# A recurrence and its mixture of experts on one core: half of the products of v moved between two PE groups, a DRAIN of GpSimd before the last four scatters, and the last output group in two column halves

## The chip, the core and the metric

One NeuronCore of a Trainium2 chip runs the whole kernel. The metric is device time in microseconds of one execution. The kernel before took 394.21 us (median of 11 runs, 393.25 to 394.7).

PE is TensorE (PEld its weight loads), DVE is VectorE, ACT is ScalarE, POOL is GpSimd, SP is SyncE. A letter q behind an engine's name (POOLq, SPq) means its sequencer: waits, branches, drains and DMA issues, which are not counted as busy time.

## The reference

A gated linear recurrence feeds a top-1 mixture of experts. Everything is float32.

```python
# q, k, v, f_logit: (4, 8, 768, 48)
f = 1.0 / (1.0 + np.exp(-f_logit))
for t in range(S):
    state = f[:, :, t, :, None] * state + np.einsum('bhd,bhe->bhde', k[:, :, t], v[:, :, t])
    y[:, :, t] = np.einsum('bhd,bhde->bhe', q[:, :, t], state)
# y -> x of (3072, 384); w_gate (384, 8), w1 (8, 384, 1024), w2 (8, 1024, 384)
...
logits = x @ w_gate
expert_idx = np.argmax(logits, axis=1)
...
h = np.maximum(x_sorted[lo:hi] @ w1[e], 0.0)
y_sorted[lo:hi] = h @ w2[e]
...
return (gate_w[:, None] * y).astype(np.float32)
```

So each of 3072 tokens gets 384 values from the recurrence, picks one of 8 experts, passes that expert's two layers, and its row is scaled by its gate and written to its own place in the output.

## The kernel before, in words

**The recurrence** is cut into chunks of 128 tokens; 12 units (`NU`) of two batch halves each are taken through a software pipeline, the loop `for n in range(1, NU + 2)`. In step `n` the unit `here = n` gets its scores, `back = n - 1` gets its outputs and `last = n - 2` is turned into token rows. The whole kernel is recorded under a manual schedule: the order in which the code emits instructions is the order in which each engine runs them. In a steady step PE runs, in this order:

- `score` (L529): 16 products k by q of unit n, into `s`
- `keys` (L544): 8 transposes of k of unit n, into two PSUM tiles `kp`; ACT copies them to `kn` (`keep`, L549)
- `rows` (L649): 8 products of the finished outputs `ys` of unit n-2 with a selection matrix, into two PSUM tiles `xp`. The tiles of `kp`, `xp` and `dp` come from two buffers used in turn (`turns`), so the first `xp` can only start when ACT has copied the first `kp`. DVE then sums the gate logits from `xp` (L657), and ACT copies the rows out (`lay`, L674 and L679)
- `within` (L557), called for `a = 0` and `a = 1`: 8 products each of masked scores `at` and `v` of unit n-1, into `yt`
- `added` (L594): 16 products of v and `kn`, into `dp`
- `before` (L578): 16 products of q and the old state, into `yt`

Beside PE, per step, DVE masks the scores (L535), scans the log decays (L477, `sum`), sums logits (L657), scales q (L518), does the routing (L214 to L260) and adds the state (L611). ACT copies `yt` out (`settle`, L619), takes exponentials and logs (L462, L470, L491, L506) and lays the rows. POOL scales k (L495), scales the state (L613), and issues the scatters of rows into the DRAM tensor `xs` (L189), sorted by expert. Every float32 product is two passes on PE, so 8 products show as 16 MATMUL records.

**The experts** follow: for each expert, a wide layer (L316, `hps`, with ReLU on ACT L326 or DVE L328) and a narrow one (L332, `yps`), in tiles of 128 tokens; DVE scales each finished tile by the gate (L344, `ysb`) and POOL scatters its 128 rows into the output (`put`, L339; `scatter`, L189). Overflowing tokens are packed into quads, four groups of 32 tokens of four experts, whose products (L1091) use four 32-column strips of PE side by side. The last expert ends in this order: the tile that rides with a quad (`narrow_riding`), the load of the last quad's second weights (`quad_second`), DVE's 16 transposes for the last quad (`turn_quad`, L1084), two plain tiles (`narrow_late`), and the last quad (`narrow_quad` with `last` set), whose gate scaling is shared by DVE (columns 192 to 383, L344) and ACT (columns 0 to 191, L346), before one scatter of it.

**The end**: a register is loaded (L1151) and a branch (L1152) skips the fallback code. POOL's sequencer then runs INC_SWDGE_SEM (L1152) and a DRAIN (L1300); SP's waits for all semaphores, the last scatter's among them (L1300); then all engines meet in two barriers.

Of the kernel before, what the change touches and what calls it, by code (L numbers as in the profile page):

```python
# [10 lines left out]
F32 = mybir.dt.float32  # L11
I32 = mybir.dt.int32
U8 = mybir.dt.uint8
AF = mybir.ActivationFunctionType
# [11 lines left out]
NU = B // 2 * NC  # L26
# [99 lines left out]
def kernel(  # L126
# [211 lines left out]
            )  # L338
        put(x, t, yp, group)  # L339

    def put(x, t, yp, group, last=False):
        ysb = ep.tile([128, DM], F32, name="ysb")
        gate, half = x["tg"][:, t, 1:2], DM // 2 if last else 0
        nc.vector.tensor_scalar(ysb[:, half:], yp[:, half:], gate, None, op0=OP.mult)  # L344
        if last:
            nc.scalar.activation(ysb[:, 0:half], yp[:, 0:half], AF.Copy, scale=gate)  # L346
        scatter(out, x["dst"][:, t : t + 1], ysb, N - 1, group)


    ordered = {getattr(mybir.EngineType, n) for n in ENGINES}  # L350
# [56 lines left out]
    with ExitStack() as st:  # L407
# [107 lines left out]
        def by_decay(u, part=whole):  # L515
            x = units[u]
            q = x["q"][:, part]
            nc.vector.tensor_tensor(q, q, x["dec"][:, part], op=OP.mult)  # L518
# [270 lines left out]
        for n in range(1, NU + 2):  # L789
            here, back, last = n, n - 1, n - 2  # L790
            ahead = n + 1 < NU
            state = n < NU - 2
            rt = None
            if here < NU:
                units[here]["old"] = states[here % 2]
            if 2 <= last:
                settle(last)
            if later and later[0] < NU - 1:
                later[1].weigh()
            if here < NU:  # L800
                for a in range(2):
                    score(here, a)
            if ahead and n != 2:
                by_r(n + 1)
                ends(n + 1)
            if decayed:
                decayed()
                decayed = None
            if sends:
                scatter_some(n)  # L810
            if n == NU - 2:
                soon = [load_rows(first[e]) for e in range(EARLY)]
            if n == 1:
                units[0]["old"] = None
                added(0)
                update(0)()
            if ahead and not 1 < n < 4:
                decay(n + 1)
                last_decay(n + 1)
            if state:  # L820
                keys(here)
                keep(here)
            if n == 2:
                growth(n + 1)
                by_r(n + 1)
                ends(n + 1)
            if 1 < n < 4:
                decay(n + 1)
                last_decay(n + 1)
            if here < NU:  # L830
                for a in range(2):
                    for h in range(2):
                        mask(here, a, h)
            if n == 1:
                log(3)
                within(0, 0)
                within(0, 1)
                settle(0)
            if n + 3 < NU:
                steps(n + 3)  # L840
            if later and n >= NU - 1:
                settled(*later)
                later = None
                scatter_some(NU)
            if 2 < n < NU - 2:
                total(n + 2)
            if n == NU - 2:
                by_decay(n + 1)
            if 0 <= last:
                rt = rows(last, later[1] if later else None)  # L850
                lay(last)
            if later and n == NU - 2:
                settled(*later)
                later = None
                scatter_some(NU)
            if ahead and n < NU - 2:
                by_decay(n + 1)
            if n == 2:
                total(n + 2)
            if rt:  # L860
                rt.choose()
                if n < NU - 2:
                    routed.append(rt.latest)
                if n >= NU - 1:
                    rt.weigh()
            if later:
                settled(*later)
                routed.append(later[1].latest)
                later = None
            for a in range(2):  # L870
                if 0 < back < NU:
                    within(back, a)
            if n == 2:
                settle(1)
            if n + 2 < NU and n != 1:
                growth(n + 2)
            if n == NU + 1:
                widen(soon[0], weights[0], early_h, range(3, 7))
            if n == NU:
                turn_early(soon[0])  # L880
            if state:
                added(here)
                decayed = update(here)
            if n == 1:
                total(3)
            if back < NU:
                before(back)
            if rt:
                later = (n, rt)
                if n >= NU - 1:  # L890
                    rt.count(turns("rp", [128, 2, rt.n, E]))
                if n >= NU:
                    settled(*later)
                    later = None
            if n == NU:
                early_h = early_banks()
                widen(soon[0], weights[0], early_h, range(3))
            if n == NU + 1:
                widen(soon[0], weights[0], early_h, range(7, NF))
                turn(soon[1])  # L900
            if n == 1:
                load(n + 3, "q")
            if n + 3 < NU:
                load(n + 3, "k")
            if n + 2 < NU:
                load(n + 2, "v")
            if 1 < n and n + 3 < NU:
                load(n + 3, "q")
            if n + 5 < NU:
                load(n + 5, "f")  # L910
            if n == 1:
                load_first_pads()
            if n in (8, 10):
                load_first_weights((n - 8) // 2)
                load_second_weights((n - 8) // 2)
# [106 lines left out]
    with ExitStack() as st:  # L1022
# [27 lines left out]
        def quad_second(q, g):  # L1050
            quads[q]["second"][g] = w2 = qp.tile([128, NF, DM], F32, name="qw2", bufs=4)
            quad_weights(w2, q, g, moe_w2, W2)
# [30 lines left out]
                for j, to in pieces():  # L1083
                    nc.vector.transpose(x["hT"][to, :, r], hq[r, j])  # L1084

        def narrow_pieces(parts, x, t, last=False):

            yp = psz.tile([128, DM], F32, name="yps")
            for f in range(NF):
                for (g, r), (h, at, w) in zip(pieces(), parts):  # L1090
                    nc.tensor.matmul(  # L1091
                        yp[r],
                        lhsT=h[:, f, at : at + T],
                        rhs=w[:, f],
                        start=f == 0,
                        stop=f == NF - 1,
                        skip_group_check=True,
                    )
            put(x, t, yp, "out", last)

        def narrow_quad(x, last):
            narrow_pieces([(x["hT"], g * T, x["second"][g]) for g in range(4)], x, 0, last)

        def narrow_riding(x, w, ridden, g):

            t = TILES - 1
            parts = [(x["hT"], t * C + j * T, w[1]) for j in range(3)]
            narrow_pieces([*parts, (ridden["hT"], g * T, ridden["second"][g])], x, t)

        quads = [None] * QUADS  # L1110

# [8 lines left out]
        for e in range(E):  # L1120
            x, w = rows_of[e], weights[e]
            end = e == E - 1
            x["hT"] = qp.tile([128, NF, TILES * C], F32, name="hT")[:, :, 0 : x["rows"]]
            widen(x, w, bank, range(NF))
            if e in WITH:
                widen_quad(quads[WITH[e]])
            if e + 1 < E:
                turn(rows_of[e + 1])
            if e + 1 in WITH:
                turn(quads[WITH[e + 1]], qp)  # L1130
            if e + 2 < E:
                rows_of[e + 2] = load_expert(e + 2)
                load_first_weights(e + 2)
            fetch(2 * e)
            if e in WITH and not end:
                turn_quad(quads[WITH[e]])
            if end:
                narrow_riding(x, w, quads[0], RIDE[e])
                quad_second(1, 3)
                turn_quad(quads[WITH[e]])  # L1140
            for t in range(TILES - 1 if e in RIDE else x["n"]):
                narrow_late(x, t, w)
            if end:
                narrow_quad(quads[WITH[e]], True)
            elif e in RIDE:
                narrow_riding(x, w, quads[0], RIDE[e])
            if e + 2 < E:
                load_second_weights(e + 2)
            fetch(2 * e + 1)
# [155 lines left out]
```

## Time and profile before

| what | value |
|---|---|
| runs shown | 394.21 us median, 393.25 to 394.7 |
| profiled execution | 394.03 us, span of its instructions 392.2 us |
| mean granted TensorE clock | 0.992 |
| busy: PE, PEld, DVE, ACT, POOL | 375.7, 263.3, 168.5, 103.1, 113.5 us |
| 25 scatters into the output, POOL | 971 ns each |
| 24 scatters into `xs`, POOL | 1293 ns each on average |

The profile gives instructions in groups (line, engine, operation, output and inputs, shapes), each group's busy time, its mean duration and the idle time of its engine before it with what ended that. `[0.24 <-ACT kn L549]` behind a row of the timeline says that the engine stood idle for 0.24 us and that ACT's copy into `kn` ended that. PE ends are modelled; PE starts are recorded. The recurrence takes the first 120 us or so, the experts the rest.

### The profile page before, as it was taken

What the parts mean: (1) busy time and instruction counts of PE and PEld (TensorE: products, weight loads), DVE (VectorE), ACT (ScalarE), POOL (GpSimd) and SP (SyncE); (2) the same over time, 40 slices, a digit from 0 to 9 for tenths busy, and PEclk for the clock granted to TensorE, in tenths of its full rate; (3) what the DMA queues carried; (4) which work ended last, traced back from release to release, by engine and by line L of the source; (5) the groups of instructions that cost most, each with busy time, mean ns of one, the idle gap of its engine ahead of it and who ended that gap; (6) DMA issues with size and microseconds to landing.
All of it is one profiled execution on the core that took longest, in us unless ns stands there. A gap on an engine that the chain in (4) does not pass through costs nothing. (4 is left out here: it accounts for less than half of the span.)

```text
span 392.2 us, 7597 instructions
## 1 busy us (share of the span) xinstructions
PE 375.7 (96%) x2998; PEld 263.3 (67%) x2998; DVE 168.5 (43%) x362; ACT 103.1 (26%) x191; POOL 113.5 (29%) x117
## 2 busy tenths in 40 slices
PE   7889999999999999999999999999999999999991
PEld 7778889999989778685555555655466466464440
DVE  6899988888664632112121131117312113011540
ACT  6998877785432101010100000010010010011000
POOL 5378867787617400100001001000200100100010
PEclk9999999999999999999999999999999999999996
DMA  7999667778759559694669799897182379991320
GB/s 273 390 375 345 229 206 250 238 238 287 277 161 357 182 147 330 147 345 77 195 203 353 237 390 395 214 399 189 40 293 63 99 274 389 406 403 51 117 106 24
DMA packets 51484, 95.05 MB, mean 242 GB/s; under 512 B 20802, under 2 KB 40696, under 8 KB 49392
## 3 DMA queue, kind: packets, MB, share of 16 engines
q1 hardware_dynamic: 48016, 84.76, 64.2%
q0 software_dynamic: 3136, 9.64, 6.5%
q8 instruction: 25, 0.41, 0.4%
q14 instruction: 19, 0.16, 0.1%
q10 hardware_dynamic: 288, 0.08, 0.1%
HBM read 79.46 MB, written 15.21 MB: 241 GB/s over the span
## 5 line engine op out<-in xcount | busy, mean ns | idle before, releaser
L316 PE MATMUL hps<-xT,w1t 128*128 128x352 f32 (+2 forms) x384 | 110.1, 447 | 0.0
L316 PEld LDWEIGHTS hps<-xT,w1t 128*128 128x128 f32 x384 | 72.7, 190 | 37.2 <-issue 1.9
L332 PE MATMUL yps<-w2t,hT 128*128 128x384 f32 x288 | 94.4, 487 | 0.0
L189 POOL DMA_INDIRECT out_dram<-ysb,dst x25 | 24.3, 971 | 229.1 <-DVE ysb L344 224.2
L332 PEld LDWEIGHTS yps<-w2t,hT 128*128 128x128 f32 x288 | 54.6, 190 | 38.5 <-issue 1.5
L326 ACT ACTIVATE hT<-hps 128x352 f32<-128x352 f32 (+2 forms) x28 | 13.7, 490 | 200.7 <-PE hps L316 190.6
L328 DVE TENSOR_SCALAR hT<-hps 128x352 f32<-128x352 f32 (+2 forms) x28 | 15.6, 558 | 93.0 <-PE hps L316 93.0
L344 DVE TENSOR_SCALAR ysb<-yps,tg 128x384 f32<-128x384 f32 x22 | 13.6, 618 | 74.5 <-PE yps L332 55.8
L189 POOL DMA_INDIRECT xs<-xr,posi x24 | 31.0, 1293 | 16.7 <-DVE place L245 9.6
L535 DVE COPY_PREDICATED at<-mpack,s 128x512 f32<-128x512 uint8 x48 | 31.0, 725 | 9.4 <-PE s L529 9.4
L495 POOL TENSOR_TENSOR k<-k,r 128x1024 f32<-128x1024 f32 (+1 forms) x12 | 26.5, 2212 | 22.1 <-ACT r L491 10.4
L477 DVE TENSOR_TENSOR_SCAN sum<-g,cap 128x1032 f32<-128x1032 f32 (+1 forms) x14 | 28.7, 2053 | 3.0 <-ACT g L470 3.0
L649 PE MATMUL xp<-fpack,ys 128*128 128x104 f32 x192 | 25.2, 281 | 2.6 <-ACT kn L549 2.4
L1091 PE MATMUL yps<-qw,hqT 128*32 128x384 f32 x128 | 26.7, 488 | 0.0
L529 PE MATMUL s<-q,k 64*128 64x128 f32 x384 | 24.7, 278 | 2.1 <-POOL last L513 1.5
L649 PEld LDWEIGHTS xp<-fpack,ys 128*128 128x128 f32 x192 | 22.7, 192 | 4.8 <-ACT kn L549 4.3
L529 PEld LDWEIGHTS s<-q,k 64*128 64x128 f32 x384 | 22.4, 188 | 4.0 <-POOL last L513 1.6
L557 PE MATMUL yt<-at,v 128*48 128x128 f32 x384 | 23.5, 275 | 0.0
L1091 PE MATMUL yps<-w2t,hT 128*32 128x384 f32 x192 | 21.4, 487 | 0.0
L557 PEld LDWEIGHTS yt<-at,v 128*48 128x48 f32 x384 | 20.4, 123 | 1.3 <-issue 0.2
L518 DVE TENSOR_TENSOR q<-q,g 128x1024 f32<-128x1024 f32 (+1 forms) x14 | 16.7, 1196 | 0.5 <-DMA q<-in_qu_dram 0.5
L619 ACT COPY ys<-yt 128x512 f32<-128x512 f32 x24 | 12.9, 591 | 14.2 <-PE yt L578 14.2
(113 smaller groups left out, 351.6 us busy)
## 6 DMA issues: line engine op xcount, KB each, us to landing
qw<-in_moe_w_dram SPq DMA_DIRECT2D x16, 1536.0 KB, 12.8
w1t<-in_moe_w_dram SPq DMA_DIRECT2D x8, 1536.0 KB, 6.8
w2t<-in_moe_w_dram SPq DMA_DIRECT2D x8, 1536.0 KB, 14.3
k<-in_ku_dram SPq DMA_DIRECT2D x12, 512.0 KB, 5.4
q<-in_qu_dram SPq DMA_DIRECT2D x12, 512.0 KB, 4.9
f<-in_fu_dram SPq DMA_DIRECT2D x11, 512.0 KB, 6.1
xs<-pad SPq DMA_DIRECT2D x8, 600.0 KB, 4.3
v<-in_vu_dram SPq DMA_DIRECT2D x12, 384.0 KB, 5.3
```

The source lines that it names most:

```text
L189: ins = nc.gpsimd.indirect_dma_start(out=dst, out_offset=bass.IndirectOffsetOnAxis(ap=idx, axis=0), in_=src, in_offset=None, bounds_check= ...
L316: nc.tensor.matmul(x["h"][:, f], lhsT=w[0][:, j, b * 128 : b * 128 + 128], rhs=x["xT"][:, j], start=j == 0, stop=j == KD - 1,)
L328: nc.vector.tensor_scalar(to, x["h"], 0.0, None, op0=OP.max)
L332: nc.tensor.matmul(yp, lhsT=x["hT"][:, f, t * C : t * C + C], rhs=w[1][:, f, :], start=f == 0, stop=f == NF - 1,)
L477: nc.vector.tensor_tensor_scan(x["sum"][:, part].rearrange("p s c -> p (s c)"), x["g"][:, part].rearrange("p s c -> p (s c)"), cap[:, part ...
L495: ins = on.tensor_tensor(k, k, units[u]["r"][:, part], op=OP.mult).ins
L518: nc.vector.tensor_tensor(q, q, x["dec"][:, part], op=OP.mult)
L529: nc.tensor.matmul(ps[h][:, p], lhsT=x["k"][r, s], rhs=x["q"][r, s], start=True, stop=True)
L535: nc.vector.copy_predicated(x["at"][:, a, h], _bc(causal, 1, HP), x["ps", a][h])
L557: nc.tensor.matmul(x["yt"][DP * (h ^ a) : DP * (h ^ a) + D, a, p], lhsT=x["v"][:, a, 2 * p + h], rhs=x["at"][:, a, h, p], start=p == 0, st ...
L649: nc.tensor.matmul(xp[:, p], lhsT=x["ys"][:, a, p], rhs=wx[:, p, 0:XW] if a else wx[:, p, E:WX], start=True, stop=True,)
L1091: nc.tensor.matmul(yp[r], lhsT=h[:, f, at : at + T], rhs=w[:, f], start=f == 0, stop=f == NF - 1, skip_group_check=True,)
```

## The change

Three edits. (1) In steps 2 to 9 `within(back, 0)` is called after `keys`, ahead of `rows`, and `within(back, 1)` stays where both were. (2) A plain DRAIN is put in POOL's stream behind the scatter of the last riding tile, ahead of the four scatters that then remain (two plain tiles and two halves). (3) The last quad is multiplied in two column halves of 192, each with its own PSUM tile, its own gate scaling on DVE, its own SBUF tile (`ysh`, a pair of buffers) and its own scatter into the output seen as 6144 rows of 192; ACT's part is gone. The two lists of destinations (`dst2`) are made by two small DVE operations just ahead of the 16 transposes of `turn_quad`. No instruction of SP is added or moved.

```diff
-    def put(x, t, yp, group, last=False):
+    def put(x, t, yp, group):
         ysb = ep.tile([128, DM], F32, name="ysb")
-        gate, half = x["tg"][:, t, 1:2], DM // 2 if last else 0
-        nc.vector.tensor_scalar(ysb[:, half:], yp[:, half:], gate, None, op0=OP.mult)
-        if last:
-            nc.scalar.activation(ysb[:, 0:half], yp[:, 0:half], AF.Copy, scale=gate)
+        nc.vector.tensor_scalar(ysb, yp, x["tg"][:, t, 1:2], None, op0=OP.mult)
         scatter(out, x["dst"][:, t : t + 1], ysb, N - 1, group)
+
+    HD = DM // 2
+    out_halves = out.rearrange("n (h d) -> (n h) d", h=2)
+
+    def halves_of(x, t):
+
+        x["dst2"] = ep.tile([128, 2], I32, name="dst2", bufs=1)
+        with nc.allow_low_precision("whole numbers"):
+            for h in range(2):
+                nc.vector.tensor_scalar(
+                    x["dst2"][:, h : h + 1], x["tg"][:, t, 0:1], 2.0, float(h), op0=OP.mult, op1=OP.add
+                )
+
+    def put_half(x, t, h, yp, group):
+        ysb = ep.tile([128, HD], F32, name="ysh")
+        nc.vector.tensor_scalar(ysb, yp, x["tg"][:, t, 1:2], None, op0=OP.mult)
+        scatter(out_halves, x["dst2"][:, h : h + 1], ysb, 2 * N - 1, group)
...
+            first_half = 1 < n < NU - 2
+            if first_half:
+                within(back, 0)
             if 0 <= last:
                 rt = rows(last, later[1] if later else None)
                 lay(last)
...
-            for a in range(2):
+            for a in range(int(first_half), 2):
                 if 0 < back < NU:
                     within(back, a)
...
-        def narrow_pieces(parts, x, t, last=False):
-
-            yp = psz.tile([128, DM], F32, name="yps")
+        def narrow_pieces(parts, yp, cols=slice(0, DM)):
...
-                        rhs=w[:, f],
+                        rhs=w[:, f, cols],
...
-        def narrow_quad(x, last):
-            narrow_pieces([(x["hT"], g * T, x["second"][g]) for g in range(4)], x, 0, last)
+        def narrow_quad(x):
+            parts = [(x["hT"], g * T, x["second"][g]) for g in range(4)]
+            for h in range(2):
+                yp = psz.tile([128, DM], F32, name="yps")[:, 0:HD]
+                narrow_pieces(parts, yp, slice(h * HD, h * HD + HD))
+                put_half(x, 0, h, yp, "out")
...
             if end:
                 narrow_riding(x, w, quads[0], RIDE[e])
+                nc.gpsimd.drain()
                 quad_second(1, 3)
+                halves_of(quads[WITH[e]], 0)
                 turn_quad(quads[WITH[e]])
             for t in range(TILES - 1 if e in RIDE else x["n"]):
                 narrow_late(x, t, w)
             if end:
-                narrow_quad(quads[WITH[e]], True)
+                narrow_quad(quads[WITH[e]])
```

More of the change, by code (lines that the diff above doesn't have):

```diff
@@ L1098, in narrow_pieces @@
                     )
-            put(x, t, yp, "out", last)
-        def narrow_quad(x, last):
-            narrow_pieces([(x["hT"], g * T, x["second"][g]) for g in range(4)], x, 0, last)
+        def narrow_quad(x):
[4 more added lines that the diff above has]
+                put_half(x, 0, h, yp, "out")
         def narrow_riding(x, w, ridden, g):
@@ L1107, in narrow_riding @@
             parts = [(x["hT"], t * C + j * T, w[1]) for j in range(3)]
-            narrow_pieces([*parts, (ridden["hT"], g * T, ridden["second"][g])], x, t)
+            yp = psz.tile([128, DM], F32, name="yps")
+            narrow_pieces([*parts, (ridden["hT"], g * T, ridden["second"][g])], yp)
+            put(x, t, yp, "out")
         quads = [None] * QUADS
```

## The prediction, made before the changed kernel ran

> **What bounds the kernel now.** I read the page first, then the list of waits, then one steady step of the recurrence in the timeline, then the end. PE is the bound nearly everywhere:
>
> ```profile
> PE 375.7 (96%) x2998; PEld 263.3 (67%) x2998; DVE 168.5 (43%) x362; ACT 103.1 (26%) x191; POOL 113.5 (29%) x117
> ...
> PE   7889999999999999999999999999999999999991
> ```
>
> Only the first slices and the last one are open. In the list of waits PE's largest wait between those is the one that edit 1 aims at:
>
> ```profile
> PE xp L649 <- ACT kn L549: 2.4, 8, 0.7
> ```
>
> Eight times in the recurrence, 2.4 us in all, the row products stand until ACT has copied the transposed keys. One steady step, number 7:
>
> ```profile
> 73.33 2.59 DVE L535 COPY_PREDICATED at<-mpack,s 128x512 f32<-128x512 uint8 x4 [1.35 <-PE s L529]
> ...
> 74.12 1.09 PE L544 MATMUL kp<-fpack,k 128*128 128x128 f32 x8
> ...
> 75.45 2.03 PE L649 MATMUL xp<-fpack,ys 128*128 128x104 f32 x16 [0.24 <-ACT kn L549]
> ...
> 77.42 1.96 PE L557 MATMUL yt<-at,v 128*48 128x128 f32 x32
> 78.03 0.26 DVE L657 TENSOR_REDUCE lg<-xp 128x8 f32<-128x32 f32 x2
> 78.21 1.21 DVE L518 TENSOR_TENSOR q<-q,g 128x1024 f32<-128x1024 f32 x1
> ...
> 79.20 1.09 PE L594 MATMUL dp<-v,kn 128*64 128x48 f32 x32
> ...
> 80.75 2.36 POOL L495 TENSOR_TENSOR k<-k,r 128x1024 f32<-128x1024 f32 x1 [1.28 <-DVE ex L222]
> 81.24 0.94 PE L529 MATMUL s<-q,k 64*128 64x128 f32 x12
> ```
>
> The step is 9.1 us from score to score (72.14 to 81.24), PE stands for 0.24 of it, and DVE (1.35) and POOL (1.28) wait longer than that: PE sets the pace. The end:
>
> ```profile
> 378.07 5.37 PE L1091 MATMUL yps<-qw,hqT 128*32 128x384 f32 x64
> ...
> 383.51 0.42 DVE L344 TENSOR_SCALAR ysb<-yps,qtg 128x192 f32<-128x192 f32 x1 [4.71 <-PE yps L1091]
> 383.96 0.42 ACT L346 ACTIVATE ysb<-yps,qtg 128x192 f32<-128x192 f32 x1 [23.41 <-DVE ysb L344]
> 384.66 0.97 POOL L189 DMA_INDIRECT out_dram<-ysb,dst  x1 [4.61 <-ACT ysb L346]
> ```
>
> ACT's half runs behind DVE's, not beside it. After PE's last pass (383.44) there are still 8.7 us, and the chain view, which knows no sequencers, stops at the last scatter. What follows is in the source view of the program's last line and of the scatter:
>
> ```profile
> L1300 POOLq DRAIN  x3: 40/248/4077, 386.8 to 391.9; - x3
> ```
> ```profile
> DMA to landing us min/median/max: 4.1/4.1/4.1
> ```
>
> The first line: POOL's sequencer begins a DRAIN at 386.80 that takes 4.08 us, to 390.88; the barriers behind it end at 392.17, 1.29 later. The second: the last scatter landed 4.1 after its start, at 388.73; the two before it took 2.6 each. SP works off its waits 0.98 after that landing (389.71). So POOL's DRAIN ends last, by 1.17, and SP's wait for the last landing is the next limit.
>
> **Edit 1, the products of v.** Sixteen passes go from behind the row products to before them. I count by PE starts in the single records. Now: last key transpose to first row pass 0.51; row to v passes 0.205; 32 v passes 1.68 from first to last start; 0.10 to the next group. Together 2.495. After: transposes to v passes 0.20 (as in step 1, where they stand so); 16 v passes 0.79 (seven pair steps of 0.111); v to row passes unknown, 0.20 like other changes of tile shape; 0.205; 0.79; 0.10. Together 2.285: **0.21 a step**. Here a rule speaks against the edit: the Trainium skill, "TensorEngine Tiling (Array Packing)", Key Properties, says that a change of tiling mode drains TensorE. The trace prices it: row passes follow transposes of the same shape at 0.11, and a change of shape costs 0.20. There are two more changes per step. Without the rule the edit would give 0.40 a step; with it 0.21; if the unknown one cost 0.4 instead, nothing.
>
> In steps 2 and 3 the gain goes elsewhere: there `dp` waits for ACT's copy of the rows (33.17 after 0.50, 41.85 after 0.38), in step 2 because ACT has no gap before it, in step 3 because DVE hasn't. PE arrives earlier and waits longer: zero. So six steps, 4 to 9: **1.27 us**. Bounds: 0 and 2.4 (all of the wait). What is late next: the rows end 0.69 later within a step. In steps without routing counts that ends just at DVE's scan (to 78.11), costing DVE 0.1; in those with counts, 0.5. DVE's waits before its masks are 0.93 to 1.46, and POOL's before k at least 1.28, so this is covered. Its price when not is a rival below. From 120 us on PE has no wait above 0.2, so the gain reaches the end. The masks of unit n-1 and v lie a step back, and `settle` of `yt` ends at 73.35, before the new place at 75.2.
>
> **Edit 3, halves.** PE: 128 passes of 192 columns for 64 of 384. The last quad's four strips step at 0.322 for 384 columns. Four-strip groups at 128 columns (L578) step at 0.11, so 192 columns should step at about 0.165, 32 steps: 5.3 against 5.15 now, within 0.1. Per four, 0.13 of weight loads fits inside. Both ends: 5.15, and 10.3 if a step stayed at 0.322; I take the near one because 128 columns already run at a third. DVE and POOL for the first half fall at about 381 to 382.6, beside PE. Their PSUM tiles are freed by DVE at 376 and 378.8, in time. For the second: PE ends at 383.44, DVE 0.42 at 383.51, POOL 0.28 after DVE as before: the last scatter starts at **384.21 instead of 384.66**. ACT's half and its handover are gone. The two small DVE operations (0.13 each by the casts L305) delay the transposes by 0.26; they end at 375.4 and PE wants them at 378.07.
>
> **Edit 2, the DRAIN.** First its own time: POOL has 6.77 idle between the riding tile's scatter (ends 369.56) and the next (376.33). If the DRAIN waits for that scatter's landing (374.74), or takes 4.08 from 369.6, it is over before 376. It has no releasers and no user. Were it stretched as scatters are beside DVE (2.33 instead of 0.97) it would end at 379.4, pushing two scatters by 3 and 1 us, whose landing nobody waits for before 386. So zero, up to about 15 us.
>
> Then the last DRAIN. What makes it 4.08 no row says outright. Three more DRAINs on POOL: 0.19 at the start, no DMA issued yet; 0.25 and 0.04 right after the long one, POOL idle in all. So the time belongs to what happened since the previous DRAIN: 49 scatters, 0.083 each. It isn't the last landing, which came 2.15 before its end. If it is work per scatter, four remain: 0.33. If it is a fixed price once any scatter was issued, 4.08 stays. The rule: the Trainium skill, "VectorE: DVE Perf Modes", section "The DRAIN you can't avoid", counts DRAINs of pre- and postamble as about 12 ns boilerplate on all engines. SP's rows agree (7 to 13 ns), POOL's row exceeds it 340 times, so the row decides. By the rule there is nothing to win here; by the row up to 3.7.
>
> **The sum at the end.** Last scatter 384.21, landing 2.6 later (the two rows before it; the 4.1 of the last one had one packet behind a 16 KB instruction fetch from 386.04 to 387.67 on its ring, and the new packets start at 385.75, ahead of that): 386.81. POOL: scatter to 385.18, INC_SWDGE_SEM 1.16, a DRAIN of 0.3 or until the landing: 387 at most. SP: 386.81 + 0.98 = 387.79, which is now the later. Plus 0.04 and 1.29: 389.12, **3.05 less** than 392.17. With 1.27: 4.32. The profiled execution was 394.03 (span 392.17 and 1.86 around): 389.71. It lies 0.18 below the median of the runs, so **389.9**.
>
> **Rivals.** (a) The DRAIN is shortened, but the last landing again meets an instruction fetch and takes 4.1: plus 1.5, 391.4. For it: fetches come as engines reach the end, which moves little against the scatter. (b) The DRAIN's price is fixed: POOL ends 386.37 + 4.08 + 1.29 = 391.74, 0.43 less, with edit 1 1.7: 392.5. For it: nothing counts the scatters in any row; against: the short ones right behind. (c) Slower: the rows' delay of 0.69 passes through DVE (logits, q, state) into the next score, in every step from 2 to 9. That costs 8 x 0.69 = 5.5 instead of gaining 1.27: 394.21 - 3.05 + 5.5 = 396.7. It decides from 0.5 a step on, (3.05 + 0.8) / 8; against it stands the 0.93 and more that DVE waits for PE now. (d) The change doesn't do what it says: DRAIN fixed and the shape changes eat edit 1: 0.43, 393.8.
>
> **Chances.** Forecast 0.50 (389.2 to 390.7), (a) 0.18, (b) 0.18, (c) 0.07, (d) 0.07. A difference of 0.2% (0.8 us) is about what this kernel's runs can tell from none. Faster: forecast, (a), (b), 0.86; within: (d), 0.07; slower: (c), 0.07. The range 389.1 to 392.9 holds the first three with their spread.
>
> **What would show it.** Edit 1: the wait of `xp` for `kn` gone, steps 4 to 9 at 8.9 instead of 9.1, PE's 120 us mark 1.3 earlier. Edit 3: the halves end 5.2 to 5.4 after their start, last scatter 0.77 after PE. Edit 2: a DRAIN of some 4 to 5 us near 370 and under 1 us at the end. I am wrong if the last DRAIN is still 4, if steps stay at 9.1, or if the halves take far over 5.4.

## The result and the profile after

The changed kernel takes **390.11 us** (median of 8 runs, 389.79 to 390.56) against 394.21 for the kernel before beside it (31 runs): a ratio of 0.9899, 95% interval 0.9888 to 0.9911, so 3.5 to 4.4 us less. Its profiled execution took 390.09, its span 388.3, at a granted clock of 0.996.

The page's busy row and its slices of PE:

```profile
PE 375.9 (97%) x3062; PEld 264.6 (68%) x3062; DVE 168.5 (43%) x365; ACT 103.0 (27%) x190; POOL 113.8 (29%) x118
...
PE   7889999999999999999999999999999999999993
```

PE is as busy as before (375.7), in 64 more records; the last slice went from a tenth to three, since less lies behind PE's end. PE's list of waits (engine, line, for whom: us in all, times, longest):

```profile
PE yt L708 <- DVE gsum L433: 2.1, 1, 2.1
PE s L543 <- POOL last L527: 1.4, 1, 1.4
PE xp L663 <- DMA fpack<-in_moe_w_gate_dram: 1.1, 1, 1.1
PE dp L608 <- ACT xr L693: 0.8, 1, 0.8
PE s L543 <- POOL rend L515: 0.5, 1, 0.5
PE xp L663 <- ACT ys L633: 0.2, 1, 0.2
```

The eight waits of `xp` for `kn` are gone. What is left comes once each, at the start of the recurrence or at its end; `dp` waits 0.83 in step 3 for ACT's rows, where 0.38 stood before. Step 7 in the timeline:

```profile
72.61 2.62 DVE L549 COPY_PREDICATED at<-mpack,s 128x512 f32<-128x512 uint8 x4 [0.60 <-PE s L543]
73.41 0.86 PEld L558 LDWEIGHTS kp<-fpack,k 128*128 128x128 f32 x8
73.41 1.09 PE L558 MATMUL kp<-fpack,k 128*128 128x128 f32 x8
...
74.43 1.08 PE L571 MATMUL yt<-at,v 128*48 128x128 f32 x16
...
75.14 2.28 DVE L491 TENSOR_TENSOR_SCAN sum<-g,cap 128x1032 f32<-128x1032 f32 x1
75.24 3.04 POOL L189 DMA_INDIRECT xs<-xr,posi  x1 [0.15 <-issue]
...
75.44 2.03 PE L663 MATMUL xp<-fpack,ys 128*128 128x104 f32 x16
...
77.41 1.08 PE L571 MATMUL yt<-at,v 128*48 128x128 f32 x16
...
80.19 2.37 POOL L509 TENSOR_TENSOR k<-k,r 128x1024 f32<-128x1024 f32 x1 [0.30 <-DVE ex L222]
80.35 0.49 PE L543 MATMUL s<-q,k 64*128 64x128 f32 x4
```

From score (71.42) to score (80.35) the step takes 8.93 instead of 9.10, without a gap on PE. The slack that covered the edit has shrunk: DVE waits 0.60 before its masks instead of 1.35, POOL 0.30 before `k` instead of 1.28. In step 9, 0.17 is left of DVE's 0.93. The end of the timeline:

```profile
376.07 0.97 POOL L189 DMA_INDIRECT out_dram<-ysb,dst  x1 [7.86 <-issue]
...
376.72 5.41 PE L1107 MATMUL yps<-qw,hqT 128*32 128x192 f32 x128
...
379.60 0.42 DVE L360 TENSOR_SCALAR ysh<-yps,qtg 128x192 f32<-128x192 f32 x1 [2.15 <-PE yps L1107]
380.29 0.97 POOL L189 DMA_INDIRECT out_dram<-ysh,dst  x1 [1.60 <-DVE ysh L360]
382.20 0.42 DVE L360 TENSOR_SCALAR ysh<-yps,qtg 128x192 f32<-128x192 f32 x1 [2.18 <-PE yps L1107]
382.89 0.97 POOL L189 DMA_INDIRECT out_dram<-ysh,dst  x1 [1.63 <-DVE ysh L360]
```

PE ends at 382.13 (383.44 before), and the last scatter starts 0.76 later. The two DRAINs, in the source views of their lines (duration min/median/max in ns, then first and last start), and the landing of the two half scatters, in the view of tile `ysh`:

```profile
L1160 POOLq DRAIN  x1: 8202/8202/8202, 367.0 to 367.0; - x1
```
```profile
L1323 POOLq DRAIN  x3: 46/249/2039, 384.2 to 388.0; - x3
```
```profile
DMA to landing us min/median/max: 2.2/2.7/3.1
```

The new DRAIN takes 8.20, not 4. The last one takes 2.04 instead of 4.08: it starts at 384.17, the last scatter lands (the last of the 16 counts of its semaphore comes) at 385.99, 3.1 after the scatter's start, and the DRAIN ends at 386.20, 0.21 behind that landing. SP has worked off its waits at 387.04, so SP, by way of the landing, now ends last, and the barriers behind it end at 388.32.

Where the 3.85 us of span went: 1.31 ahead of PE's end, 2.54 behind it (8.73 before, 6.19 after). Of the 1.31, 0.38 was there at the first score of the pipeline already (9.93 and 9.55), ahead of any edit. Steps 0 to 2 added 0.11, and step 3 took 9.98 instead of 9.70 with the wait of `dp`, a loss of 0.28 that the repeat below doesn't have (9.69). So at the score of step 4 the changed kernel was 0.21 ahead (43.95 and 43.74); in the repeat, whose first score came at 9.20, it was 0.01 ahead (43.94). Steps 4 to 9 gave 0.17 each, 1.02, and the rest came behind them.

### The profile page after: what moved, and what is told of

It reads as the page before. It is cut to its first block, busy times and chain, and to the rows that moved or that the text cites. A ratio compares the mean times of both kernels' runs of the same rounds, so it can differ in the third digit from the quotient of the medians.

```text
span 388.3 us, 7726 instructions
## 1 busy us (share of the span) xinstructions
PE 375.9 (97%) x3062; PEld 264.6 (68%) x3062; DVE 168.5 (43%) x365; ACT 103.0 (27%) x190; POOL 113.8 (29%) x118
## 4 chain that ended last, share of the span: by engine, by line
PE 89%; DMA 5%; SPq 1%; DVE 1%; ACT 1%; issue 1%; POOL 0%; POOLq 0%; ACTq 0%
PE hps L316 28%; PE yps L332 24%; PE yps L1107 7%; PE xp L663 6%; PE yt L571 5%; PE s L543 5%; PE s L316 3%; PE hps L1081 3%; PE yp L332 3%; PE yt L592 3%; PE dp L608 2%; DMA fpack<-c_fpack 2%; PE kp L558 2%; DMA f<-in_fu_dram 2%; DMA fpack<-in_moe_w_gate_dram 2%; SPq L466 1%
## 5 line engine op out<-in xcount | busy, mean ns | idle before, releaser
L189 POOL DMA_INDIRECT out_dram<-ysb,dst x24 | 23.3, 972 | 224.4 <-DVE ysb L343 216.3
L189 POOL DMA_INDIRECT xs<-xr,posi x24 | 32.3, 1347 | 16.6 <-DVE sums L235 9.2
L1107 PE MATMUL yps<-qw,hqT 128*32 128x192 f32 (+1 forms) x192 | 26.8, 380 | 0.0
L571 PE MATMUL yt<-at,v 128*48 128x128 f32 x384 | 25.1, 277 | 0.0
L1107 PEld LDWEIGHTS yps<-w2t,hT 128*32 128x32 f32 x192 | 7.6, 110 | 13.0 <-issue 12.5
```

The lines of the kernel that those rows point to most:

```text
L189: ins = nc.gpsimd.indirect_dma_start(out=dst, out_offset=bass.IndirectOffsetOnAxis(ap=idx, axis=0), in_=src, in_offset=None, bounds_check= ...
L571: nc.tensor.matmul(x["yt"][DP * (h ^ a) : DP * (h ^ a) + D, a, p], lhsT=x["v"][:, a, 2 * p + h], rhs=x["at"][:, a, h, p], start=p == 0, st ...
L1107: nc.tensor.matmul(yp[r], lhsT=h[:, f, at : at + T], rhs=w[:, f, cols], start=f == 0, stop=f == NF - 1, skip_group_check=True,)
```

## Experiments

Two things were open. **Edit 1**: how much of the gain is its own, and is it covered by slack. **The DRAIN**: the forecast read 4.08 us as 49 scatters at 0.083 each, but the new DRAIN with 46 scatters behind it took 8.20. My first theory for that: it waits for the last landing and then takes 0.043 per scatter (386.80 to 390.88 holds both). Rivals: 0.083 per scatter from its own start, stretched by DVE's transposes beside it in the new place; or a fixed price.

The first and the third batch ran on two chips whose granted TensorE clock falls to 0.5 for 7 to 10 us near 122 us in all eight kernels profiled there (in two of them, the first run of edit 1 alone and both halves ahead, also for 3.4 us, from 31.3 and from 35.5), and the kernel before takes 403.9 and 403.74 us there. So times are compared within a batch, and the tail (from PE's last end to the span's end) across batches. The changed kernel itself was run only where there is no such fall.

**Edit 1 alone** (first batch)

```diff
--- before
+            first_half = 1 < n < NU - 2
+            if first_half:
+                within(back, 0)
...
-            for a in range(2):
+            for a in range(int(first_half), 2):
```

> Only the move of the first half of the products of v (edit 1). Theory of the record: steps 4 to 9 each 0.17 to 0.21 us shorter, nothing in steps 2 and 3: 394.2 - 1.0 to 1.3 = 392.9 to 393.2. Rival: the profile of the changed kernel has step 3 longer by 0.28 us and a start that was 0.4 us earlier by itself; if the move causes the longer step 3, the gain is 0.7 or less: 393.5. The end of the kernel is as before: the DRAIN of 4 us sets it.

403.87 us, ratio 0.9989 (0.9974 to 1.0004); tail 8.74. A gain of at most 1 us, and none shown: the 1.0 to 1.3 that were expected aren't there. Its even steps are 9.38 as in the changed kernel, but steps 5, 7 and 9 are 9.23 to 9.28 instead of 8.93: the 32 passes of `before` (L578, `yt<-q,state`) take 1.1 to 1.2 from first to last start instead of 0.82.

**Edit 2 alone** (first batch)

```diff
--- before
                 narrow_riding(x, w, quads[0], RIDE[e])
+                nc.gpsimd.drain()
                 quad_second(1, 3)
```

> Only the DRAIN ahead of the last expert's remaining scatters (three here, edit 2). Theory now: a DRAIN waits for the last scatter's landing and then takes about 0.043 us for each scatter since the DRAIN before (before: 2.15 us after the landing for 49; changed: 1.92 for 46, 0.21 for 4). The last one then ends 0.15 to 0.25 us after the landing, SP's waits 1.0 after it, and the end comes 1.1 us earlier: 393.1. Rival, the record's reading: 0.083 us for each scatter from its own start; the same end, but the DRAIN in the middle takes 3.8 us, not 8. Rival, a fixed price: 394.2.

402.88, ratio 0.9973 (0.9953 to 0.9993); tail 7.61, 1.12 shorter. The line of its last DRAIN, in the source view:

```profile
L1301 POOLq DRAIN  x3: 46/249/3054, 395.5 to 400.4; - x3
```

It still has 3.05, but as a wait for the landing (398.37, 0.17 ahead of its end), which now sets the end through SP.

**Edit 3 alone** (first batch)

```diff
--- changed kernel
-            first_half = 1 < n < NU - 2
+            first_half = False
...
-                nc.gpsimd.drain()
```

> Only the last quad in two column halves (edit 3), no DRAIN and no move. The last scatter starts 0.45 us earlier. Theory now (landing, then 0.043 us for each of 50): the DRAIN at the end still takes long and ends 2.15 us after the last landing, so the whole gain of the landing counts, 0.45 plus what the landing itself gets shorter (4.1 down to 2.6 to 3.1): 1.4 to 1.9, 392.3 to 392.8. Rival, the record's 0.083 for each scatter from the DRAIN's own start: only the earlier start counts, 0.45, 393.8.

403.65, ratio 0.9989 (0.9968 to 1.0009); tail 8.36, 0.37 shorter.

```profile
L1322 POOLq DRAIN  x3: 40/249/4158, 395.9 to 401.1; - x3
```

Fifty scatters, 4.16 us from its start at 395.91 to 400.07. The counts of the last scatter's semaphore, kept in the trace, put its landing at 396.98: a landing followed by 0.043 per scatter would have ended the DRAIN at 399.13, 0.94 sooner. That theory falls here.

**Edits 1 and 3** (first batch)

```diff
--- changed kernel
-                nc.gpsimd.drain()
```

> The changed kernel without its DRAIN. Theory now: the last DRAIN again ends about 2.15 us after the last landing, SP's waits 1.05 after it, so 1.1 us slower than the changed kernel: 391.2. Rival: the DRAIN buys nothing (its price is fixed, or the landing sets the end anyway): 390.1. Rival 0.083 us from its own start: the DRAIN would begin near 384.2 and end at 388.3, where the changed kernel's ended at 386.2: 391.3, not to be told apart by the time, but by the DRAIN's end against the landing.

403.48, ratio 0.9983 (0.9965 to 1.0001); tail 8.36, DRAIN 4.16 again, 2.80 of it behind the landing. The second miss of that theory.

**The changed kernel again** (second batch, before 393.91)

> The changed kernel once more, beside the others on one chip. Theory now: the DRAIN takes 0.083 us for each scatter since the DRAIN before, from its own start, and ends no earlier than 0.2 after the last landing (49 scatters 4.08, 50 scatters 4.16, wherever the landing was). So 1.1 us or a little more less than without its DRAIN, and 3 to 4 us less than before. Rival: on the chip of the single edits the steps 5, 7 and 9 lost 0.3 us each in the products with the old state, with edit 1 only; if that is the chip's doing, edit 1 is worth 0.2 to 0.4 there and the changed kernel only 2 to 2.5 us less than before.

390.46 (390.16 to 391.21), ratio 0.9912 (0.9897 to 0.9928); tail 6.32. The result repeats, with 3.45 between the medians instead of 4.10.

**Edits 2 and 3** (second batch)

```diff
--- changed kernel
-            first_half = 1 < n < NU - 2
+            first_half = False
```

> The changed kernel without edit 1 (DRAIN and halves alone). Theory: the tail gain of 2.5 to 3.0 us alone, so 391.2 to 391.7 where before is 394.2, and 1.0 slower than the changed kernel beside it. Rival: edit 1 is worth nothing or 0.3, then it is within 0.3 of the changed kernel. DRAIN without halves gave 0.8 to 1.1 and halves without DRAIN 0.35 to 0.45; if these were all, the pair would give 1.2 to 1.5; the theory has more for the pair, since without the long DRAIN the earlier landing counts too.

391.98, ratio 0.9942 (0.9924 to 0.9961); tail 6.35. Against the changed kernel beside it edit 1 is worth 0.0030 of the ratio, 1.2 us, or 1.5 by the medians; steps 9.55 and 9.10 against 9.38 and 8.93 account for 1.02. The two intervals just touch, so the runs alone leave the size of it loose.

**The DRAIN far ahead, 26 scatters left** (second batch)

```diff
--- changed kernel
         over, okc = share(), sums()
+        nc.gpsimd.drain()
...
-                nc.gpsimd.drain()
```

> The changed kernel with its DRAIN at the end of the recurrence instead, behind the 24 scatters into xs, so that 26 scatters are left for the last one. Theory (0.083 each, from its own start, not before the landing): the last DRAIN takes 26 x 0.083 = 2.16, starts 1.3 after the last scatter and ends 3.5 after its start, about 0.4 after a landing at 3.1; SP's waits end 1.05 after the landing, so the time is that of the changed kernel. Rival (landing, then 0.043 each): DRAIN ends 1.1 after the landing, no more than 0.1 slower. Rival (two prices, 4 us when anything is left from the recurrence's scatters, else 0.3): also the time of the changed kernel, but the DRAIN ends with the landing plus 0.2. The first DRAIN, 24 scatters: 2.0 of work, or until the landing of the last row plus 0.2.

391.0, ratio 0.9928 (0.991 to 0.9947), which the runs can't tell from the changed kernel beside it; tail 6.14.

```profile
L1323 POOLq DRAIN  x3: 46/248/2368, 385.3 to 388.7; - x3
```

It starts at 385.33, the last scatter lands at 386.59, it ends at 387.70: 1.11 after the landing, 0.043 for each of 26. By 0.083 from its own start it would have been 387.49; in the changed kernel (four scatters) the end follows the landing by 0.21, in the long new DRAINs (46) by 1.93. The new DRAIN of this kernel has 24 scatters behind it:

```profile
L1014 POOLq DRAIN  x1: 7839/7839/7839, 129.6 to 129.6; - x1
```

It takes 7.84 where 2.0, or the landing and 0.2, were expected: the landing comes at 136.44, and it ends 1.03 later, 0.043 for each of 24.

**The DRAIN away from the transposes, edit 1 in steps 4 to 9 only** (second batch)

```diff
--- changed kernel
-            first_half = 1 < n < NU - 2
+            first_half = 3 < n < NU - 2
...
+            if end:
+                nc.gpsimd.drain()
             x["hT"] = qp.tile([128, NF, TILES * C], F32, name="hT")[:, :, 0 : x["rows"]]
...
-                nc.gpsimd.drain()
```

> The changed kernel with edit 1 in steps 4 to 9 alone, and the DRAIN at the start of the last expert, 45 scatters behind it and 5 ahead, where DVE makes no transposes. Theory: in the changed kernel the DRAIN in the middle ended 1.9 us after the landing because DVE's 16 transposes ran beside it; here its 45 x 0.083 = 3.7 us are over before the landing (7 us after the scatter), and it ends within 0.3 of it. Rival: it ends 1.9 after the landing here too (45 x 0.042 after it). Time: edit 1 gave nothing in steps 2 and 3 but 0.3 more in step 3, so 0 to 0.3 faster than the changed kernel; the earlier DRAIN changes nothing at the end.

390.29 (389.93 to 390.62), ratio 0.9903 (0.9887 to 0.9919); tail 6.13.

```profile
L1145 POOLq DRAIN  x1: 9086/9086/9086, 342.4 to 342.4; - x1
```

With DVE nearly idle (busy for 1.05 of these 9.1 us) and 45 scatters behind it, the DRAIN takes 9.09 and ends 1.89 after the landing. So the transposes have no part in its length. Leaving steps 2 and 3 as before makes no difference that shows (390.29 against 390.46).

What fits all of these DRAINs, as a sum and not as something that a row shows: **two passes of about 0.0415 us per scatter issued since the last DRAIN, and the second starts only when the last of them has landed**, so end = later of (start + 0.0415 n, landing) + 0.0415 n. Before: 386.80 + 2.03 = 388.83, just behind the landing at 388.73, + 2.03 = 390.86 (measured 390.88). The walk of 0.083 from its own start fits there only because the landing came within the first half. Every scatter here has 128 rows, so a price per scatter and a price per row can't be told apart; the size of a row doesn't show (49 scatters of whole rows and 50 with two of half rows both give 0.0832 each). The third batch tests this on a new place.

**The DRAIN between the last two plain tiles** (third batch)

```diff
--- changed kernel
-                nc.gpsimd.drain()
                 quad_second(1, 3)
...
                 narrow_late(x, t, w)
+                if end and t == 0:
+                    nc.gpsimd.drain()
```

> The changed kernel with its DRAIN moved two places back in time, between the scatters of the two last plain tiles: 47 scatters lie before it, three after, and DVE's 16 transposes are over. Theory of two passes (0.0415 us per scatter, the second pass only once the last scatter has landed): the DRAIN ends 1.95 us after the later of start + 1.95 and the landing, some 3.9 to 4.3 us after its start, and the last DRAIN of three ends 0.2 after its landing. Rival, a walk of 0.083 per scatter from the landing: 3.9 after the landing. Rival, that the 8.2 us of the DRAIN in the changed kernel come of the transposes beside it and the place is free of cost: 3.9 from its start, with the landing of no matter. The three scatters behind it are held: by the first theory the last one starts at most 0.4 later than in the changed kernel and the time is 0 to 0.5 us above it.

402.19, ratio 0.997 (0.9949 to 0.999).

```profile
L1166 POOLq DRAIN  x1: 5118/5118/5118, 386.1 to 386.1; - x1
```

From 386.08 to 391.20, 5.12 where 3.9 to 4.3 were expected. The landing of the last scatter ahead of it, by the counts of its semaphore, is at 388.88. The sum as it stands gives 388.88 + 1.95 = 390.83, 0.37 too early; a walk of 0.083 from the DRAIN's start gives 389.98, from the landing 392.78. So none of the three holds as it was written. But the row of that scatter runs from 386.31 to 387.29, beyond the DRAIN's own start. With the first pass begun at the end of that row the sum is 387.29 + 1.95 + 1.95 = 391.19. That start was fitted to this one run and not tried on another; in the other DRAINs it changes nothing, since at the end the scatter's row is over before the DRAIN begins, and in mid-kernel the landing comes later than the first pass. With it, all 23 DRAINs of over 1 us in the 14 traces end 0.01 to 0.05 behind the sum. The scatters behind it were held (the second plain tile's to 392.07). The last one started at 395.64, but not for that alone: DVE's second half began at 394.94, 1.9 after PE's last recorded start instead of the 0.40 of the changed kernel, for a reason that no row shows (PE's semaphore, for which DVE waits, comes only at 394.92). So the price of this place isn't settled by the trace.

**Both halves of v ahead of the rows** (third batch)

```diff
--- changed kernel
                 within(back, 0)
+                within(back, 1)
...
-            for a in range(int(first_half), 2):
+            for a in range(2 * int(first_half), 2):
```

> The changed kernel with both halves of the products of v ahead of the row products in steps 2 to 9 (the change has one half there). PE then has as many changes of tile shape as before edit 1 (transposes to v, v to rows, rows to dp: three, one fewer than in the changed kernel), and the rows end another 0.9 us later within a step. My theory, that edit 1 gains because PE has work while ACT copies the keys, and loses only the shape changes: one change and one v-to-v gap fewer, so a step of 8.8 to 8.95 us as long as DVE's slack of 0.9 to 1.4 us covers the delay; the time within 0.8 us of the changed kernel, the logits of DVE running 0.9 later in the step. The rival of the record, the rows' delay passing through DVE into the next score: steps with routing counts (5, 7, 9) become longer than 9.2, with a wait of PE's score or state group for DVE or ACT behind it, and the whole is 1 to 5 us slower than the changed kernel.

402.51, ratio 0.996 (0.994 to 0.9981), 0.3 to 0.4 above the two other kernels with the shortened tail in this batch, which the runs can't tell from none. In the trace it is plain: even steps 9.39, no better than 9.38, and steps 5, 7 and 9 at 9.77, 9.48 and 9.57 where edit 1 alone has 9.28, 9.19 and 9.22 on this chip. Its list of waits has the reason:

```profile
PE dp L608 <- ACT xr L693: 3.3, 4, 2.2
```

`dp` waits 0.4 in each of steps 5, 7 and 9, in the first two for ACT's copy of the rows, which waits for DVE's logits (the view names no releaser in step 9; the 2.2 is in step 2). DVE has no wait before its masks left in these steps. So DVE's slack holds one half of the products, and not two. The gain that I expected from one shape change fewer didn't come: in step 4 the change of groups saved is worth 0.10, but 32 v passes in a row take 1.68 instead of twice 0.81, and the 32 passes of `dp` 0.92 instead of 0.87.

**Edit 1 alone, once more** (third batch; the edit is that of its first run)

> Edit 1 alone, once more, beside the kernel before on this chip. By the steps of the traces (0.17 us in each of steps 4 to 9) it gains 1.0 us, by the difference of the two kernels that differ in it alone on another chip 1.5: so 0.8 to 1.6 below the kernel before, with steps 5, 7 and 9 at 8.93. The rival, that the three odd steps are 0.3 us longer whenever edit 1 stands without the early DRAIN (9.22 to 9.29, as in its first run): a gain of 0.1 to 0.3 only. The tail behind PE's last product stays 8.7 us by both, the last DRAIN 4.08.

403.44, ratio 0.999 (0.9971 to 1.0009); tail 8.75, DRAIN 4.08. Steps 5, 7 and 9 are 9.28, 9.19 and 9.22 again. But the tie to the missing early DRAIN, which the expectation's rival names, is wrong: the two kernels of this batch that have a DRAIN ahead of the end and edit 1 as here have 9.19 to 9.24 too. The longer odd steps go with these two chips and edit 1 together; edits 2 and 3 alone had none in the first batch. On these chips steps 4 to 9 give 3 x 0.17 - 3 x 0.13, about 0.1 in all, which agrees with the two runs of edit 1 alone. Their cause stays open: `yt<-q,state` starts on time and loses 0.26 to 0.36 from about its tenth pass on (the view says "issue", which is no releaser), and the granted clock in the records is 1.0.

**Three column parts of 128** (third batch)

```diff
--- changed kernel
-    HD = DM // 2
-    out_halves = out.rearrange("n (h d) -> (n h) d", h=2)
+    HD = DM // 3
+    out_halves = out.rearrange("n (h d) -> (n h) d", h=3)
...
-            for h in range(2):
+            for h in range(3):
```

> The changed kernel with the last quad in three column parts of 128 instead of two of 192, each with its own scatter. The last part's scaling on DVE and its scatter are smaller: the last scatter starts 0.7 instead of 0.77 us after PE's last product. If PE steps 128 columns at a third of 384 as it does elsewhere, the tail is 0 to 0.3 us shorter and the time 0 to 0.4 below the changed kernel, which the runs may not resolve. If instead each scatter costs the same whatever its size (1 us of POOL, and one third more packets to land), the parts queue on POOL or the landing is no earlier, and the time is the same or up to 0.5 above.

402.08, ratio 0.9963 (0.9941 to 0.9985): the same as its neighbours. DVE's part shrinks to 0.35 and the scatter follows DVE's start by 0.62 instead of 0.69, but each scatter still takes 0.97, the last lands 3.1 after its start, and PE stalled inside the parts (0.56 and 0.33). None of the variants here is shown to beat the changed kernel.

## Why the prediction held, and where it didn't

The forecast of 389.9 was 0.2 off the median, and in the profiled executions 3.94 was saved where the sum had 4.32. The large terms were those that it named, edit 1's wait and POOL's long DRAIN, but the rule for the DRAIN was wrong and part of the closeness is luck. The end fell short by 0.51 and edit 1 by 0.25; the 0.21 by which this execution was ahead at step 4, which no edit made, gave some of that back. The repeat, without it, lies 0.6 above the forecast. Of the signs that the prediction named, the wait of `xp`, the shorter steps, the time of the halves and the start of the last scatter came; the two of the DRAIN did not: 8.20 near 370 instead of 4 to 5, and 2.04 at the end instead of under 1.

**Edit 1.** The step was to gain 0.21 and gained 0.17. Counted again by PE starts: transposes to v 0.202, 16 passes 0.809, v to rows 0.202 (the unknown change of shape: 0.20 was right), rows to v 0.205, 0.809, to the next group 0.102. Together 2.329 against 2.500 now. The term that was too small is 16 passes at 0.79 (0.809), twice. A change of shape doesn't always cost 0.20: in the same step v to `dp` takes 0.10 and `dp` to `yt` 0.15. "Zero" for steps 2 and 3 held in step 3 of the repeat, where `dp` waits 0.54 instead of 0.38; step 2 varies from 9.27 to 10.04 in the traces of one chip, with the loads, and tells nothing. The Trainium skill's warning ("TensorEngine Tiling (Array Packing)", Key Properties: a change of tiling mode drains TensorE) was rightly in the sum as two times 0.09 (0.20 where 0.11 stands without a change). The rows' delay through DVE, rival (c), was covered as said, in step 9 with 0.17 to spare; the kernel with both halves ahead shows the cover end, from 0.4 a step, by way of ACT's copy and not of the next score.

**Edit 3.** The groups of four step at 0.163 (0.165 predicted), so PE takes 5.41 by the page where the whole took 5.37, and the last scatter starts 0.76 behind PE (0.77). Alone it is worth 0.37 of tail: 0.48 earlier, less 0.08 for one more scatter in the long DRAIN and 0.03 in INC_SWDGE_SEM.

**Edit 2, the new DRAIN.** This step failed in size: "over before 376" was right (375.20), "takes 4.08" or "until landing" was not, since the landing (373.28) and a walk behind it (1.93) come in turn. It held the next scatter until 376.07, about 1 us later than its data allowed, and nobody waited. Of the cover named, POOL's idle time didn't last; that nobody reads those scatters before the end did.

**Edit 2, the last DRAIN.** "It isn't the last landing" held for that DRAIN by a narrow margin: its first pass ended at 388.83, the landing had come at 388.73. It was wrong as a rule, since the second pass waits for the landing. The consequence held: with four scatters the second pass is 0.17 and the landing is left, 2.04, of which 1.82 is the wait. "Under 1 us" missed that wait. INC_SWDGE_SEM, taken as 1.16 still, fell to 0.27; as POOL isn't the last any more, it bought nothing.

**The end sum.** 3.05 was predicted, 2.54 came. The 0.5 is the landing: 2.6 was taken from the two scatters ahead, and it was 3.1 here and 3.0 to 3.3 in the four of the second batch, which all have halves and a shortened last DRAIN. So rival (a) was right by a third. The packets in the traces show where it comes from. In the kernel before, the last four packets of the scatter began at 387.65, as the 16 KB instruction fetch ended (387.67). In the changed kernel no 16 KB fetch falls among these packets, but one of 8 KB does, from 384.32 to 384.82: one packet begins at 384.81, two more follow it until 385.53, and the landing comes at 385.99. In those four, too, a late packet begins within 0.02 of the end of such a fetch. That the fetch holds it is read from these times; no run moved the fetch. That SP's wait for the landing would be the next limit was right. It also explains why the parts don't add up: the DRAIN alone gives 1.12 (1.17 lay between POOL's end and SP's), the halves alone 0.37, since the DRAIN still ends last, and both together 2.4 to 2.5, since the halves' earlier start and shorter landing (3.1 instead of 4.1) count only once POOL is out of the way.

What isn't settled: edit 1 is worth 1.0 by the steps and 1.2 to 1.5 by the runs on one chip, and next to nothing on two others, whose odd steps lose 0.3 for a cause that no row shows. What the whole change is worth on those two was not measured.

## What to carry to other kernels

A duration that divides neatly by a count is not yet a price per item: find a second instance of the same instruction with another count and another place before you move it, and look at what lay halfway through it. Where two engines end within a microsecond or so of each other, work out the end as the later of the two: removing one cause then pays only the gap, and the second edit is worth more beside the first than alone. When an edit spends slack, read how much is left afterwards; here half of the moved products fitted and all of them didn't.

## What the runs showed of the hardware

- A DRAIN of POOL costs about 0.083 us per scatter (of 128 rows) issued since the last DRAIN, in two halves, the second of which starts no earlier than the landing of the last scatter: 4.08 for 49, 4.16 for 50, 2.37 for 26 and 2.04 for four, the last almost all wait. In the middle of the kernel it took 7.8 to 9.1, because landings come later there, 6.3 after the DRAIN's start in the changed kernel; 5.1 in the one place where the landing came 2.8 after its start.
- INC_SWDGE_SEM at the end grows in the same way: 1.16 with 49 scatters since the last DRAIN, 0.71 with 26, 0.27 with four.
- A scatter of POOL that starts beside DVE's scan ends only 0.8 to 0.9 behind the scan's end. In step 7 of the kernel before, the first scatter started ahead of the scan and took 1.04, the second ran beside it and took 2.33 (to 78.89, the scan ended at 78.11); in the changed kernel the first starts just after the scan does and takes 3.04 (75.24 to 78.28, the scan from 75.14 to 77.42), the second 1.11. It cost PE nothing here.
